# A gated mix of a diagonal state-space layer and a long convolution: taps taken two to a product on half-width tiles, two state tiles placed earlier, C's last tiles loaded ahead of the row loads

## The chip, the cores and the metric

One core of a Trainium2 chip runs the kernel. The metric is the device time of one launch in microseconds; 398.35 us is the median of three runs of the kernel before (398.08 to 398.38). Engines are named as in the profile: PE multiplies matrices (PEld is its weight load), DVE is the vector engine, ACT the scalar engine, POOL the general engine that here mostly issues adding DMAs, SP the engine that issues the plain and the transposing DMAs.

## The reference

The sequence has 2048 steps of 1024 channels. The output is `g * a + (1 - g) * b` with a gate `g` per step. All tensors are bf16 in and out.

```python
x = A_x
g = _sigmoid((x * gate_w).sum(-1, keepdims=True))
# a: diagonal complex state-space layer
for t in range(L):
    h = Lam_bar[None, :] * h + Bu[:, t, :]        # Bu = x @ B_bar^T
y = 2.0 * einsum("blp,dp->bld", hseq, Cmat).real + x * Dskip
# b: k is filtered with 4 taps per channel, multiplied by v, and convolved over the whole length
for t in range(ks):
    k_shift = k_shift + k_pad[:, t:t + S, :] * shift_k[:, ks - 1 - t][None, None, :]
kv = k_shift * v
y = irfft(rfft(kv_pad) * rfft(kf_pad))[:S] + kv * ssm_D
return q * y                                       # q is x
```

The state `h` is complex and has 1024 channels; its recurrence runs over all 2048 steps. `Cmat` is turned first (multiplied by a complex factor per state channel), so that the factor of `B_bar` need not be applied to `Bu`.

## The kernel before

Every instruction goes through a helper (`mm`, `tt`, `ts`, `act`, `move`, `load_t`, `gather`), and `put` fixes the order on each engine to the order in which the program calls them. All rows of the profile therefore have line 94, and they are told apart by tile names. Several sequences are written as generators, and `step` and `run` place their pieces; this is how the order of the work is written by hand.

**The convolution** goes chunk by chunk, 8 chunks of 128 channels (`c` from 0 to 7). For each chunk:

- `load` brings three tiles: `kn` (the long filter, transposed on the way in), `kT` (k transposed: channel on partitions, time along the row, `PAD` zeros in front) and `v`. `kn` and `kT` (and `v` for chunks 0 and 1) share the pool `ld` of three buffers; later `v` tiles hold two chunks each in `xt_pool`. With `held`, ACT first writes one column of the new tile, so that the DMA waits for ACT instead of for every reader of the old tile.
- `taps` computes the 4-tap filter on PE. `dgs` makes four diagonal 128 x 128 matrices, one per tap (channel factors on the diagonal). `tap_sums` takes, for each of 16 blocks of 128 time steps, four products with `kT` (shifted by 0 to 3 steps) as the weights and a diagonal matrix of 128 columns as the moving operand. ACT copies the sums to `ks`.
- `times_v` multiplies by `v` (DVE), mirrors (PE, ACT) and folds the halves (DVE `ev`, and an adding DMA `ks<-lo` from POOL).
- `fold_K`/`mirror_K`, `fwd_K`, `fwd_V` are the forward transforms on PE, copied out by ACT to `Kh` (or the free tiles `BT2`, `BT3`) and `Vh`. `products` multiplies the spectra on DVE, which is most of DVE's work there, about 23 us for a chunk. `inverse` transforms back (`psz`), and SP writes `cv` to a scratch in HBM.

The loop `for c in range(NC - 1)` works on three chunks at once: products of `c`, forward transforms of `n = c + 1`, taps of `nn = c + 2`, and loads of `c + 3`.

**The state layer** has 16 state tiles `(tb, g)`: 4 time blocks `tb` of 512 steps times 4 groups `g` of 256 state channels. `Bu(i)` makes the i-th of them in the sequence `order` from `xT` (x transposed) and `BT` (B transposed), as two halves `j` that I call half tiles; one is some 3.5 us of PE. The first four are `Bu_tile` (products `odd` and `even`, then a small correction with diagonal matrices `lamd`), the others `Bu_plain` (product `both`). Half tiles that do not depend on the convolution fill PE in the loop: 9 of the 32 lie in it, 7 in the last stage (products of chunk 7), and 16 behind it.

**The scans** follow: `scan(tb, g)` on DVE rotates, runs the recurrence, rotates back to `hb`, and adds to `U` what the odd steps lack: four products `q<-hb,lam`, then three sums (`summed`). For the last block's first three scans ACT makes the four products (`Q<-hb,lam`), and the sums are put off until the next scan's recurrence is out (`put_off`). `turn_C` turns a C tile: ACT makes `m`, DVE scales the tile twice and adds `m` (for tiles 4 and 5 an adding DMA adds it). `Cy` and `Cy_group` multiply by C (`psy`, 3.45 us for 128 rows of one group of four); the first four row blocks go row by row (`C0` to `C3`), then by group. The dict `plan` says what PE does behind each scan `j`. `loads(t)` brings a row block's `cv` and x, `scale_b` and `finish` mix it, and SP stores it.

Of the kernel before, what the change touches and what calls it, by code (L numbers as in the profile page):

```python
# [20 lines left out]
def kernel(  # L21
# [153 lines left out]
    def load(which, c, held=False):  # L175
# [7 lines left out]
        elif which == "v":  # L183

            w = 1 if c < 2 else 2
            if w == 1:
                t = ld.tile([128, NT, 1, 128], BF16, name="v", tag="ld")
            else:
                t = xt_pool.tile([128, NT, 2, 128], BF16, name="v2", tag="xT")
            move(t.rearrange("p n k d -> p n (k d)"),  # L190
                 vf.rearrange("(n p) d -> p n d", p=128)[:, :, c * 128:(c + w) * 128])
            for k in range(w):
                lds["v", c + k] = t[:, :, k]
            return
        else:

            t = ld.tile([128, PAD + S], BF16, name="kT", tag="ld")
            put("pool", nc.gpsimd.memset, t[:, 0:PAD], 0.0)
            load_t(t[:, PAD:], kf[:, cc])
        lds[which, c] = t  # L200


    kT0 = ld.tile([128, PAD + S], BF16, name="kT", tag="ld")
    v0 = ld.tile([128, NT, 1, 128], BF16, name="v", tag="ld")
    put("pool", nc.gpsimd.memset, kT0[:, 0:PAD], 0.0)
    for h in range(2):
        hs, ns = slice(h * S // 2, (h + 1) * S // 2), slice(h * NT // 2, (h + 1) * NT // 2)
        load_t(kT0[:, PAD + hs.start:PAD + hs.stop], kf[hs, 0:128])
        move(v0[:, ns, 0], vf.rearrange("(n p) d -> p n d", p=128)[:, ns, 0:128])
    lds["kT", 0], lds["v", 0] = kT0, v0[:, :, 0]  # L210
# [8 lines left out]
    def load_xT(tb, halves=(0, 1), held=False):  # L219
        if 0 in halves:  # L220
            xTs[tb] = (xt_pool if tb in (1, 2) else xt_first).tile([128, ND, TB], BF16, name="xT", tag="xT")
# [61 lines left out]
    gwb = consts.tile([128, ND], BF16, name="gwb")  # L283
    psp = ps2([128, 2, 512], "p")
# [184 lines left out]

    def of_blocks(ks, h):  # L470
# [5 lines left out]
    def taps(c, dg):  # L476
        kT = lds.pop(("kT", c))
# [204 lines left out]
    def lam_diag(g, home, on_act=False):  # L682

        t = lamd[g] = home.tile([128, 2, 3, 128], BF16, name=f"lamd{g}", tag=f"lamd{g % 2}")
# [8 lines left out]
    def Bu(i):  # L693
        tb, g = order[i]
        if i in (10, 11):
# [3 lines left out]
        else:  # L699
# [3 lines left out]
            else:  # L703
                home = uu[0 if i in (0, 1, 13, 14) else 1] if i < 6 or i in (13, 14) else s5p["uu"]
# [10 lines left out]
        return [Bu_tile(tb, g, U, j, (i, j) == (2, 1)) for j in range(2)]  # L715

    def Bu_tile(tb, g, U, j, halved):
# [3 lines left out]
        for a in (1, 0):  # L721
# [5 lines left out]
            if a == 1:  # L727
# [3 lines left out]
                if halved:  # L731
                    yield
# [42 lines left out]
    put_off = []  # L775

    def scan(tb, g, fin):
# [7 lines left out]
        for js in ([slice(0, 1), slice(1, 2)] if last else [slice(0, 2)]):  # L785
# [38 lines left out]
            by_act = tb == NTB - 1 and not last  # L824
            if by_act:
# [175 lines left out]
    old = ahead = none  # L1001
    tiles = (b for i in range(6) for b in Bu(i))

    for c in range(NC - 1):
# [6 lines left out]
        if c == 0:  # L1011
# [22 lines left out]
            load_xT(0)  # L1034
            lam_diag(0, lam_pool, True)
            continue
        if c == 1:
            load("v", 4)
# [11 lines left out]
        if c == 2:  # L1050
            load("v", 6)
        if nn < NC:
            dg = dgs(nn)
        bu = next(tiles) if c == 4 else ahead if c == 6 else none
        step(bu)
        fwd_K(n, (0, 1))
        step(bu)
        fwd_K(n, (2, 3))
        if c == 6:
            load_xT(2, held=True)  # L1060
# [18 lines left out]
        bu = [next(tiles) for _ in range({1: 1, 2: 1, 3: 1, 5: 1, 6: 3}.get(c, 0))] + [none, none]  # L1079
        if c == 5:  # L1080
            bu[1] = ahead = next(tiles)
        step(bu[0])
        fwd_V(n, (0, 1))
        if nn + 1 < NC:
            load("kn", nn + 1, True)
            load("kT", nn + 1)
        if c in (1, 2):
            load_BT(1, c - 1)
        elif c in (3, 4):
            load_xT(1, (c - 3,))  # L1090
        step(bu[0])
        step(bu[1])
        fwd_V(n, (2, 3))
        if bu[1] is not ahead:
# [265 lines left out]
```

## Time and profile before

| | |
|---|---|
| time, median of 3 | 398.35 us |
| the profiled execution: time | 400.61 us |
| the profiled execution: span from first to last instruction | 398.8 us |
| granted PE clock over the span | 0.996 |
| HBM read and written | 12.86 MB and 8.39 MB |

The share of busy time by stage, in us, from the windows of the trace:

| stage (us from the start) | length | PE | DVE | ACT | DMA share |
|---|---|---|---|---|---|
| start, chunk 0 (0 to 45) | 45 | 42.34 | 39.78 | 34.68 | 0.93 |
| loop, c = 1 to 5 begun (45 to 163) | 118 | 115.86 | 116.28 | 97.47 | 0.67 to 0.85 |
| c = 6 (163 to 187) | 24 | 23.17 | 23.90 | 16.00 | 0.69 |
| products of chunk 7 (187 to 224) | 37 | 37.00 | 36.66 | 19.57 | 0.81 |
| first scans (224 to 266) | 42 | 39.92 | 39.95 | 37.08 | 1.11 |
| scans and row blocks (266 to 394) | 128 | 127.77 | 118.86 | 82.64 | 0.75 to 1.01 |

A DMA share near or above 1 means that the 16 DMA engines had work queued throughout. Two engines, PE and DVE, are each busy nearly all of the span, and the rows must be read for which of them is waited for at a given place.

### The profile page before, as it was taken

What the parts mean: (1) busy time and instruction counts of PE and PEld (TensorE: products, weight loads), DVE (VectorE), ACT (ScalarE), POOL (GpSimd) and SP (SyncE); (2) the same over time, 40 slices, a digit from 0 to 9 for tenths busy, and PEclk for the clock granted to TensorE, in tenths of its full rate; (3) what the DMA queues carried; (4) which work ended last, traced back from release to release, by engine and by line L of the source; (5) the groups of instructions that cost most, each with busy time, mean ns of one, the idle gap of its engine ahead of it and who ended that gap; (6) DMA issues with size and microseconds to landing.
All of it is one profiled execution on the core that took longest, in us unless ns stands there. A gap on an engine that the chain in (4) does not pass through costs nothing.

```text
span 398.8 us, 6544 instructions
## 1 busy us (share of the span) xinstructions
PE 386.1 (97%) x2437; PEld 206.0 (52%) x2437; DVE 376.8 (94%) x610; ACT 287.4 (72%) x434; POOL 72.2 (18%) x96
## 2 busy tenths in 40 slices
PE   8999899999999999999999999979999999999995
PEld 5456357474656647566444444424444444444442
DVE  8799999999999999999999899999999999999944
ACT  4797995969878796765429799936978874996201
POOL 3011030200202011020001010503344233433000
PEclk9999999999999999999999999989999999999999
DMA  7969993996929398097994799978999998988402
GB/s 160 159 142 223 205 261 70 231 213 138 210 58 230 56 156 190 28 156 113 209 204 88 180 196 188 195 164 167 199 188 178 253 261 142 218 163 170 121 0 106
DMA packets 129601, 65.72 MB, mean 165 GB/s; under 512 B 106393, under 2 KB 113313, under 8 KB 129570
## 3 DMA queue, kind: packets, MB, share of 16 engines
q1 hardware_dynamic: 117664, 42.22, 48.7%
q0 software_dynamic: 11824, 23.07, 33.8%
q8 instruction: 19, 0.31, 0.3%
q14 instruction: 12, 0.10, 0.1%
q10 hardware_dynamic: 82, 0.02, 0.0%
HBM read 12.86 MB, written 8.39 MB: 53 GB/s over the span
## 4 chain that ended last, share of the span: by engine, by line
PE 68%; DVE 19%; ACT 6%; issue 4%; DMA 2%; POOL 0%; DVEq 0%; ACTq 0%; POOLq 0%
PE psy L94 27%; PE both L94 12%; PE psk L94 7%; PE taps L94 5%; PE psz L94 4%; DVE BT L94 4%; PE psv L94 3%; PE foldk L94 3%; PE even L94 3%; DVE wkh L94 3%; DVE CT L94 2%; ACT Vh L94 2%; PE odd L94 2%; DVE W L94 2%; DMA ks<-lo 2%
## 5 line engine op out<-in xcount | busy, mean ns | idle before, releaser
L94 PEld LDWEIGHTS <-BT 128*128 128x128 bf16 x640 | 62.2, 98 | 47.8
L94 PE MATMUL both<-xT,BT 128*128 128x512 bf16 x384 | 83.7, 379 | 0.0
L94 PE MATMUL psy<-CT,hb 128*128 128x512 bf16 x256 | 59.4, 387 | 2.3 <-DVE CT L94 2.3
L94 PE MATMUL psy<-CT,U 128*128 128x512 bf16 x256 | 57.4, 379 | 0.0
L94 PEld LDWEIGHTS <-hb 128*128 128x128 bf16 x256 | 25.3, 99 | 33.9 <-issue 5.1
L94 POOL DMA_DIRECT2D U<-Q x24 | 23.3, 983 | 100.8 <-ACT Q L94 61.0
L94 ACT ACTIVATE U<-both 128x512 bf16<-128x512 f32 x48 | 26.4, 593 | 20.4 <-PE both L94 20.1
L94 PEld LDWEIGHTS <-U 128*128 128x128 bf16 x256 | 25.1, 98 | 30.2
L94 ACT ACTIVATE Vh<-psv 128x1024 bf16<-128x1024 f32 x32 | 31.0, 1033 | 11.9 <-PE psv L94 11.9
L94 DVE TENSOR_TENSOR_SCAN W<-rv,init,A 128x256 bf16<-128x256 f32 x48 | 32.2, 730 | 0.0
L94 PE MATMUL taps<-dg,kT 128*128 128x128 bf16 x512 | 31.2, 223 | 0.0
L94 POOL DMA_DIRECT2D G<-wkh x8 | 9.7, 1218 | 115.5 <-DVE wkh L94 115.5
L94 PEld LDWEIGHTS <-kT 128*128 128x128 bf16 x512 | 29.8, 100 | 1.0 <-issue 0.2
L94 PEld LDWEIGHTS <-SF 128*128 128x128 bf16 x184 | 18.0, 98 | 20.0 <-issue 1.5
L94 PE MATMUL psk<-eok,SF 128*128 128x512 bf16 (+1 forms) x120 | 28.1, 354 | 0.0
L94 ACT ACTIVATE Q<-U,lam 128x512 bf16<-128x512 bf16 (+1 forms) x48 | 27.7, 606 | 0.0
L94 PE MATMUL psz<-G,CI 128*128 128x512 bf16 x64 | 24.3, 380 | 2.4 <-DVE G L94 1.9
L94 PE MATMUL psz<-G,SI 128*128 128x512 bf16 x64 | 24.3, 379 | 0.0
L94 DVE TENSOR_TENSOR wkh<-BT,Vh 128x3072 bf16<-128x3072 bf16 (+4 forms) x20 | 21.8, 1111 | 0.0
L94 DVE TENSOR_TENSOR wkh<-Kh,Vh 128x3072 bf16<-128x3072 bf16 (+2 forms) x16 | 21.3, 1350 | 0.0
L94 ACT ACTIVATE BT<-psy,gcols 128x1024 bf16<-128x1024 f32 x5 | 5.4, 1109 | 21.8 <-PE psy L94 21.8
L94 ACT ACTIVATE m<-psy,gcols 128x1024 bf16<-128x1024 f32 x8 | 8.9, 1113 | 16.6 <-PE psy L94 16.6
(189 smaller groups left out, 780.7 us busy)
## 6 DMA issues: line engine op xcount, KB each, us to landing
U<-Q POOLq DMA_DIRECT2D x24, 256.0 KB, 5.3
G<-wkh POOLq DMA_DIRECT2D x6, 768.0 KB, 8.1
cv_scr<-cv SPq DMA_DIRECT2D x16, 256.0 KB, 2.6
v<-in_B_v_dram SPq DMA_DIRECT2D x3, 1024.0 KB, 9.6
out_dram<-m SPq DMA_DIRECT2D x8, 256.0 KB, 5.6
BT<-cv_scr SPq DMA_DIRECT2D x7, 256.0 KB
out_dram<-BT SPq DMA_DIRECT2D x7, 256.0 KB, 2.0
ks<-lo POOLq DMA_DIRECT2D x6, 256.0 KB, 7.4
```

The costliest lines, as they stand in the source:

```text
L94: i = f(*a, **kw)
```

## The change

- **Taps two to a product.** For chunks 3 to 7, the channels of a chunk are split in two halves of 64. A tile then holds a half twice: on 64 partitions as it is, on the other 64 delayed by two steps. One product over 128 partitions so takes two taps of 64 channels; two products (shift 0 and 1) make the four taps, and the moving operand has 64 columns instead of 128. The number of products stays 4 for a block of 128 steps, 64 for a chunk.
- **Copies.** The second tile `kB` and the delayed halves come from three copies in SBUF, `spread`, issued by SP behind the chunk's `kT` load: two that read the fresh `kT`, and one that overwrites its upper half when these two are done. `kB` takes the third `ld` buffer.
- **Factors.** `pcol2` and `ident2` hold the factors of two taps over a half, made at the start by eight small products, a copy and a sum; `dgs` makes four matrices of 64 columns.
- **Loads.** `v` is loaded chunk by chunk into one tile `v2` for two chunks (the first of them still whole). `kn` and `v` of the next chunk are issued ahead of the taps, `kT` and the copies right behind them; `BT1` and `xT` 1 move with them, and `xT` 2 to the start of `c = 6`.
- **State tiles.** The pieces of the first four tiles (eight half tiles, three pieces each, 24 steps in all) are spread over `c` = 1 to 6, four or five pieces for each `c` (two in `c = 6`), and three half tiles of the next two lie in `c = 6`. So 11 half tiles are in the loop, 6 in the last stage (with `b10`), and the rest behind it; tile 13 moves from behind `C3` to before `C0`.
- **C.** Tiles 0 and 1 are now added by DMA too. Tiles 6 and 7 are turned inside scan 3, and loaded ahead of the rows. The order of the loads is `CT0`, `BT2`, `BT3`, `CT1`, `CT2`, `CT3`, then `CT4`, `CT5` before the inverse of chunk 7.
- **Scans 4 and 9** have their four products made by ACT, as 12, 13 and 14 had already. The products of scan 13 move behind the four copies of group `G23` on ACT.

```diff
+    def spread(c):
+        a, b = lds["kT", c], lds["kB", c]
+        lo, hi, n = slice(0, 64), slice(64, 128), PAD + S
+        move(b[lo, 8:], a[hi, 8:])
+        move(b[hi, 10:], a[hi, 8:n - 2])
+        yield
+        move(a[hi, 10:], a[lo, 8:n - 2])
...
+        for q in range(4):
+            for t in range(2):
+                mm(psp[t * 64:t * 64 + 64, 1, 64 + q * ND:64 + (q + 1) * ND],
+                   skr[:, q // 2 * 64:q // 2 * 64 + 64, q % 2 + 2 * t], ident[32:32 + ND, 32:32 + ND], True, True)
+        copy(pcol2, psp[:, 1, 64:64 + 4 * ND].rearrange("p (i j) -> p i j", j=ND))
+        tt(ident2, ident[:, 0:64], ident[:, 64:128], ALU.add)
...
+    def packed_sums(halves, dg, h):
+        ps = ps2([128, 8, 128], "taps")
+        for n in range(8):
+            for e, k in enumerate(halves):
+                for m in range(2):
+                    k0 = PAD + (8 * h + n) * 128 - m
+                    mm(ps[:, n, e * 64:e * 64 + 64], k[:, k0:k0 + 128], dg[:, e, m], m == 0, m == 1)
+        return ps
...
-            act(of_blocks(ks, h), by_block(tap_sums(kT, dg, h)), func=ACT.Copy)
+            sums = tap_sums(kT, dg, h) if c < 3 else packed_sums((kT, kB), dg, h)
+            act(of_blocks(ks, h), by_block(sums), func=ACT.Copy)
...
+    scaled_by_act = (4, 9, 12, 13, 14)
...
-            by_act = tb == NTB - 1 and not last
-            if by_act:
+            by_act = tb * NG + g in scaled_by_act
+            if tb * NG + g == 3:
+                run(turning[7])
...
     for c in range(NC - 1):
...
+        if c == 6:
+            load_xT(2)
...
             step(fk)
             if c < 5:
                 step(fk)
+            if nn + 1 < NC:
+                load("kn", nn + 1, True)
+                load("v", nn + 1)
+                if c == 1:
+                    load_BT(1, 0)
+                elif c in (2, 3):
+                    load_xT(1, (3 - c,))
+            step(parts)
             taps(nn, dg)
+            if nn + 1 < NC:
+                load("kT", nn + 1, True)
+                apart = spread(nn + 1)
+                step(apart)
+                if c == 1:
+                    load_BT(1, 1)
+                run(apart)
...
-        by_sum = pi in (4, 5)
+        by_sum = pi in (0, 1, 4, 5)
...
-    load_CT(1)
     load_BT(2, 0)
     load_BT(2, 1)
-    load_CT(2)
     load_BT(3, 0)
     load_BT(3, 1)
+    load_CT(1)
+    load_CT(2)
     load_CT(3)
...
+    CT_pool((6, 7), "ctc")
+    load_CT(6)
     loads(0)
...
-    plan = ["B8", "B9 B10", "B11", "B12 C0", "C1", "C2", "C3 B13", "B14 B15", "G10", "G11", "G12 G13", "G20", "G21",
+    plan = ["B8", "B9 B10", "B11", "B12 B13 C0", "C1", "C2", "C3 B14", "B15", "G10", "G11", "G12 G13", "G20", "G21",
             "G22 G23", "", ""]
...
+        if j == 3:
+            run(turning[6])
+        if j == 0:
+            run(turning[1])
...
-                if tl == 1 and put_off:
-                    put_off[-1][0]()
...
+    run(turning[0])
     step(scans[0])
```

More of the change, by code (lines that the diff above doesn't have):

```diff
@@ L694, in Bu @@
         tb, g = order[i]
+        if i == 13:
+            V_ = s5p["v13"].tile([128, 2, 2, HB], BF16, name="V13")
+            O_ = lam_pool.tile([128, 2, 2, HB + 2], BF16, name="O13", tag="lamd")
+            Us[tb, g] = V_, O_[:, :, :, 2:]
+            turns_U[i] = turn_U(g, V_, O_)
+            return [Bu_plain(tb, g, V_, O_, j) for j in range(2)]
         if i in (10, 11):
@@ L999 @@
     fwd_V(0, (2, 3))
-    old = ahead = none
-    tiles = (b for i in range(6) for b in Bu(i))
+    old = none
+    parts = (None for i in range(4) for b in Bu(i) for _ in b)
+    tiles = (b for i in (4, 5) for b in Bu(i))
     for c in range(NC - 1):
@@ L1049 @@
         run(old)
-        if c == 2:
-            load("v", 6)
         if nn < NC:
             dg = dgs(nn)
-        bu = next(tiles) if c == 4 else ahead if c == 6 else none
-        step(bu)
+        if c % 2 == 0:
+            step(parts)
         fwd_K(n, (0, 1))
-        step(bu)
+        if c % 2 == 0:
+            step(parts)
         fwd_K(n, (2, 3))
         if c == 6:
-            load_xT(2, held=True)
             run(sp)
@@ L1078 @@
             step(tv)
-        bu = [next(tiles) for _ in range({1: 1, 2: 1, 3: 1, 5: 1, 6: 3}.get(c, 0))] + [none, none]
-        if c == 5:
[L1081 to L1094, printed above, removed]
-            step(bu[1])
-        run(bu[2] if c == 6 else none)
-        if c == 2:
+            step(parts)
+        else:
+            run(next(tiles))
+            run(next(tiles))
+        fwd_V(n, (0, 1))
+        if c < 6:
+            step(parts)
+            if c in (1, 3):
+                step(parts)
+        fwd_V(n, (2, 3))
+        if c == 5:
+            step(parts)
+        elif c == 6:
+            run(next(tiles))
+        if c == 1:
             lam_diag(1, lam_pool)
@@ L1152 @@
         steps(prod, 3)
-        b0, b1, b2 = tiles
-        run(b0)
+        run(next(tiles))
         run(back)
         gate(1)
-        run(b1)
+        gate(2)
         run(prod)
@@ L1163 @@
         run(turns_U[6])
-        run(b2)
-        gate(2)
         steps(turning[0], 2)
@@ L1168 @@
         run(b8)
-        back = inverse(c)
-        step(back)
-        run(back)
+        steps(turning[1], 2)
         run(b9)
-        steps(turning[1], 2)
+        b10, b11 = Bu(8)
+        run(b10)
+    CT_pool((4, 5), "ctb")
+    load_CT(4)
+    load_CT(5)
+    back = inverse(c)
+    step(back)
+    run(back)
     h3.close()
```

82 lines of the change are left out of this document (51 added, 31 removed).

## The prediction

> **What bounds the kernel now.** I read the page's busy table first, then the chain of waits over the last third, then the timelines of PE and DVE where the chain names them.
>
> ```profile
> PE 386.1 (97%) x2437; PEld 206.0 (52%) x2437; DVE 376.8 (94%) x610; ACT 287.4 (72%) x434; POOL 72.2 (18%) x96
> ```
>
> Two engines fill the span, so shortening one gains only until the other ends last. The chain from 260 us on (start, length, engine and tile):
>
> ```profile
> 264.93 0.02 issue
> 264.96 1.24 DVE CT L94
> 266.19 0.04 issue
> 266.23 23.42 PE psy L94 x100
> 289.65 20.72 PE both L94 x96
> 310.37 0.78 PE p L94 x32
> 311.15 82.92 PE psy L94 x384
> 394.07 0.02 issue
> ```
>
> DVE's turned C tile releases PE at 266.23, and from there PE runs without a gap to 394.07; 4.73 us of last sums and stores follow. The 96 products `both` are six half tiles, 3.45 us each. How far behind is DVE? Its timeline:
>
> ```profile
> 226.72 0.48 DVE L94 TENSOR_SCALAR CT<-CT,c2r 128x1024 bf16<-128x1024 bf16 x1 [1.50 <-ACT m L94]
> ...
> 235.31 1.14 DVE L94 TENSOR_SCALAR q<-hb,lam 128x512 bf16<-128x512 bf16 x4
> ...
> 379.35 0.49 DVE L94 TENSOR_TENSOR hb<-hb,trn 128x256 bf16<-128x256 bf16 x2
> ```
>
> and PE's:
>
> ```profile
> 82.12 3.75 PE L94 MATMUL taps<-dg,kT 128*128 128x128 bf16 x64
> 85.71 1.91 PE L94 MATMUL odd<-xT,BT 128*128 128x256 bf16 x16
> 87.45 1.91 PE L94 MATMUL even<-xT,BT 128*128 128x256 bf16 x16
> ...
> 174.04 0.94 PE L94 MATMUL p<-gwb,xT 128*128 128x1 bf16 x32
> 174.84 1.91 PE L94 MATMUL odd<-xT,BT 128*128 128x256 bf16 x16
> ...
> 380.07 3.62 PE L94 MATMUL psy<-CT,hb 128*128 128x512 bf16 x16
> 383.53 3.62 PE L94 MATMUL psy<-CT,U 128*128 128x512 bf16 x16
> ```
>
> The last `hb` is done at 379.84, and PE begins the last group, which reads it, at 380.07: DVE is only 0.23 us ahead there. That first row block reads the second half of `hb` from its ninth product on, 8 x 0.216 = 1.73 us later. So PE can come forward by 0.23 + 1.73 = 1.96 us alone; all beyond that needs DVE earlier too. In the loop the two are level as well: inverse transforms start at 46.48, 69.63, 93.21, 117.19, 140.35 and 164.41, about 23.5 us apart, of which PE's own work is 23.15 us.
>
> **The change, part by part, for PE.** Start to start, 64 tap products take 85.71 - 82.12 = 3.59 us, 56.1 ns each; 256 columns take 1.74/16 = 109 ns, 512 columns 3.46/16 = 216 ns. That is 0.416 ns a column, so 64 columns should take 56.1 - 26.6 = 29.4 ns: 1.71 us less for a chunk, 8.5 us for five. No row has 64 columns. The bounds are nothing saved (the weight load, as long as before, sets the pace) and 56.1 - 25.0 = 31.1 ns, 9.95 us in all, from the gate's 32 products with one column and a full weight load (174.04 to 174.84, 25.0 ns each). I take 8.5, as that row puts the weight load below 29.4 ns.
>
> By the Trainium skill, "TensorE: Matmul & The Clock Gate", section "Back-to-back issue gap", a stream of weight load and product pairs sustains some 81 ns for 128 columns, set by both operations. By that the pair would be bound by its load and the change would save nothing; the trace's 56.1 ns and 25.0 ns disagree, and I go by them.
>
> The pieces take the room up. Before, `c` = 1 to 4 held one half tile each (3.5 + 0.44 = 3.94 us). Now `c` = 1 and 3 hold odd, even, correction, odd = 1.75 + 1.75 + 0.44 + 1.75 = 5.69, and `c` = 2 and 4 hold 1.75 + 0.44 + 3.94 = 6.13. With 1.71 off, PE's work there changes by +0.04 and +0.48 us: 1.0 us more over four iterations. At `c` = 5 it falls by 1.8 us and at 6 by 1.2 us. In the last stage six half tiles stand ahead of the inverse of chunk 7, as before; but now `b6` is one half tile earlier and needs `BT2`. DVE frees `BT2` at 190.5 as before, its load now follows `CT0` at once (before at 191.90), and lands some 5.1 us after a 1.9 us issue, the second part near 200. PE asks near 197 and waits 1 to 3 us, which the 1.8 us gained in the loop cover: the inverse ends near 219 (219.57 before). Eleven half tiles follow before `C0`, as before. So `C0` starts near 257 (257.56), two half tiles fewer lie behind it (6.9 us), and PE's two waits for C (1.28 and 1.03 us) go, as tiles 6 and 7 are turned within scan 3. PE could end 0.6 + 6.9 + 2.3 = 9.8 us earlier.
>
> **For DVE.** Scans 4 and 9 lose 1.14 us each (4 `q` products): 2.28. Tiles CT0 and CT1 lose the addition, 1.14 us start to start each: 2.28. The start gains a copy and a sum on the critical start, 0.17 us rows both: +0.35. Work: -4.2 us. The wait of 1.50 us for ACT's `m` of CT1 goes, since it is made before `b9` is copied out; what was late behind it was PE's `both` of 219.73, so it doesn't return elsewhere. The loop costs something back: if DVE waits for every bit that PE is longer, 1.0 us, if none, 0; I take 0.5. Sum: 4.2 + 1.5 - 0.5 = 5.2 us earlier.
>
> **Both together.** The end moves by the smaller of 9.8 and 5.2 + 1.96 = 7.16: 7.1 us. The span becomes 398.8 - 7.1 = 391.7. The profiled execution took 400.61 in all, 2.26 above the median; taking 7.1 from the median gives 391.25, and I say 391.3.
>
> **What is costed at nothing, and its cover.** SP issues 15 copies more, two more `v` loads, POOL four more adding DMAs (0.86 to 0.98 us each), ACT ten more activations in scans and holds. ACT has room (72%). On SP the copies wait for the `kT` load, and the last for the first two; behind them stand both parts of `xT` 0 at `c` = 0, the second part of `BT1` at `c` = 1, and always the two `cv` stores, whose tile is needed again 23 us later. The chain from ACT's hold to the last copy is one issue (1.96), one landing (4.6), two copies in a row (256 KB each; `pbb` 4.6): 15.8 us. Least: 1.24 + 4.1 + 2.0 + 2.0 = 9.3; most, with the folding DMA's 9.3 for a copy: 3.7 + 5.8 + 18.6 = 28.1. The cover is one iteration less taps and copy-out, 23.5 - 1.9 - 1.0 = 20.6. At 15.8 there are 4.8 us to spare, so I take nothing.
>
> The Trainium skill, "DMA: Bandwidth & Descriptors", "Specifications", asks for 512 bytes or more in one descriptor; `v` in single chunks has runs of 256. By it a half load would cost up to what a whole one did. The rows here give 4.1 us for 256 KB in 256-byte runs and 9.6 us for 1 MB in 512-byte runs, nearly in proportion to 2 x 4.1 for half the bytes, so the rule holds partly; a `v` load is needed an iteration later, and its sum stays nothing.
>
> **Rivals.**
> - *PE alone sets the end.* If DVE sheds also its small waits (0.62 us twice for `Vh`, 0.55 in the first scans), it is 7.0 us earlier, 8.9 with the half group, and the end moves 8.9 us: 389.5. For: PE is freer at c = 5 and 6. Against: it isn't at c = 1 to 4.
> - *DVE gains only its work.* If every iteration of the loop costs DVE about 0.6 us more, by pieces on ACT between the copies of `Vh`, or if ACT's products for scan 13, now behind four copies that wait for PE, hold DVE by 2 us: 7.1 - 3 = 4.1, giving 394.3. For: loop and tail have no slack on DVE.
> - *The weight load paces the taps.* Then the loop is 1.75, 2.19, 1.75, 2.19 us longer on PE, 7.9 in all, of which DVE at level pegging pays some 7: 5.2 + 0.5 - 7 + 1.96 = +0.7 gained, 397.7 to 398.3, no change. Against: 25.0 ns at the gate.
> - *The copies come late: slower.* PE stands in order before the taps of chunks 3 to 7, and each us beyond the cover costs a us five times, because DVE waits for `ks`. At 22.6 us for the chain the loss is 10 us against 7.1: 401.3. It decides from 22.0 us on (1.4 x 5 = 7.1). For: the DMA share is 1.0 to 1.3 between 30 and 60 us and 0.96 to 1.12 from 70 to 90. Against: it is 0.72 and 0.00 in the ten us after the taps at 60 to 70, just where the chain would run.
>
> **How the numbers follow.** Forecast 391.3, chance 0.53; PE alone 389.5, 0.10; DVE's work only 394.3, 0.18; no gain, 0.06; late copies, 0.13. Faster by over 0.2% (about 0.8 us, what these measurements can tell) holds in the first three: 0.81; within 0.2%: 0.05; slower: 0.14. The range runs from 388.6 (all 9.8 us) to 396.5 (DVE's work only, and two more us lost in the loop); what is left out is the last two cases.
>
> **What would show it.** Right: tap products at about 29 ns; DVE's last `hb` near 374.6 and PE's last group waiting about 2 us for it; `both` rows behind `C0` 64 instead of 96; no wait for CT around 264. Wrong: PE idle in front of `taps` with the copies of `kB` or `kT` as releaser (late copies); tap products still near 56 ns; DVE waiting for `Vh` over 3 us in the loop; a wait for `BT2` beyond 4 us at `b6`.

## The result, and the profile after

The changed kernel takes 414.25 us (median of 4, 411.55 to 418.05) beside 398.37 us of the kernel before on the same chip: 1.0368 times as long, with an interval of 1.0299 to 1.0437. The prediction was 391.3 us. The profiled execution took 413.06 us, its span is 411.3 us and the granted clock 0.973. Kernels of this study scatter by several per cent where the kernel before stays within about one; a ratio below compares undisturbed executions alone, so that it can stand lower than the medians over all runs do, and it is left out where too few were undisturbed.

The page's busy table of the changed kernel:

```profile
PE 382.3 (93%) x2411; PEld 201.5 (49%) x2445; DVE 372.0 (90%) x602; ACT 291.3 (71%) x444; POOL 76.4 (19%) x100
```

PE has 3.8 us less to do than before (386.1) and DVE 4.8 us less (376.8). DVE's work fell as forecast (4.2). PE's figure is rough, since the table lists 2411 products beside 2445 weight loads; what its taps gained is read from their starts below. The kernel is slower because both engines now stand idle: DVE for 39.3 us of the span, where it was 22.0. Where? The changed kernel's timeline for PE, at the taps of chunk 3 (columns: start, length, engine, operation, tiles, count, and in brackets the idle time ahead and who ended it):

```profile
61.10 0.22 PE L94 MATMUL taps<-dg,kT 128*128 128x64 bf16 x2
...
62.96 1.91 PE L94 MATMUL even<-xT,BT 128*128 128x256 bf16 x16
```

Sixty-four tap products from 61.10 to 62.96: 29.1 ns each. Then the next iteration, in the chain of waits of the changed kernel:

```profile
70.62 4.35 DMA kT<-in_B_k_dram
...
76.20 4.42 SPq L94
...
80.73 12.70 DMA kT<-kT
...
93.47 3.07 PE taps L94 x64
```

and PE's timeline just ahead of those taps:

```profile
91.48 1.89 PE L94 MATMUL odd<-xT,BT 128*128 128x256 bf16 x8 [5.72 <-DMA BT<-in_A_B_im_dram]
```

The load of `kT` 4, SP's issue of `BT1`'s second part and the third copy stand one behind the other, 22.8 us from the issue at 70.62 to the last landing at 93.43. The prediction's chain starts earlier, at ACT's hold of the tile, and from there it is 29.4 us, because SP is busy with the loads ahead. ACT's timeline, then SP's:

```profile
64.08 0.20 ACT L94 ACTIVATE kT<-pih 128x1 bf16<-128x1 f32 x1
```

```profile
60.59 4.54 SPq L94 DMA_TRANSPOSE kn<-in_B_ssm_k_dram  x1
...
65.81 4.65 SPq L94 DMA_TRANSPOSE BT<-in_A_B_re_dram  x1
```

PE waits for two things here, one behind the other. `BT1`, which was issued between the copies, holds it in the middle of sixteen `odd` products that began at 84.71; when they are done, the third copy has just landed. Without the wait for `BT1` PE would have reached the taps near 86.5, and the copy alone would have held it 7.0 us. At the taps of chunk 6 PE waits for the third copy itself:

```profile
143.36 0.22 PE L94 MATMUL taps<-dg,kT 128*128 128x64 bf16 x2 [1.24 <-DMA kT<-kT]
```

The windows of 10 us (PE, PEld, DVE, ACT and POOL busy, then PE clock, DMA share, GB/s), first of the kernel before:

```profile
80.00:90.00 10.00, 10.00 (x111) 7.80 (x109) 9.93 (x11) 6.62 (x9) 0.14 (x2) 1.00 0.97 211
```

then of the changed kernel:

```profile
80.00:90.00 10.00, 5.76 (x33) 2.76 (x30) 9.93 (x11) 4.93 (x7) 0.97 (x2) 0.95 1.45 133
90.00:100.00 10.00, 8.36 (x97) 6.44 (x99) 5.28 (x5) 3.55 (x5) 0.11 (x1) 0.71 1.14 236
```

Look at the last two columns together: the DMA engines are busier than before (1.45 against 0.97) and move fewer bytes (133 against 211 GB/s).

A ruler for the loop is the start of DVE's full-width product of spectra, one an iteration:

| kernel | c=0 | 1 | 2 | 3 | 4 | 5 | 6 |
|---|---|---|---|---|---|---|---|
| before | 47.47 | 71.19 | 95.18 | 118.19 | 141.90 | 165.40 | 190.43 |
| changed | 48.14 | 72.13 | 103.49 | 127.04 | 152.47 | 175.97 | 200.98 |

The shift is 0.67, 0.94, 8.31, 8.85, 10.57, 10.57, 10.55 us: 7.4 us are lost around chunk 4's taps and 1.7 around chunk 6's. Behind the loop it grows again. The timelines of ACT and DVE of the changed kernel follow; in that stretch of the kernel before DVE's longest wait is 1.50 us, and ACT waits for no load:

```profile
250.01 1.15 ACT L94 ACTIVATE pbb<-pbb,omg 128x1024 bf16<-128x1024 bf16 x1 [8.76 <-DMA pbb<-cv_scr]
252.82 1.15 ACT L94 ACTIVATE gd<-rows,gcols 128x1024 bf16<-128x1024 bf16 x1 [1.67 <-DMA rows<-in_A_Dskip_dram]
```

```profile
256.08 0.48 DVE L94 TENSOR_SCALAR CT<-CT,c2r 128x1024 bf16<-128x1024 bf16 x1 [9.59 <-ACT m L94]
```

ACT stands 8.8 us at the first row's `pbb`, with `m` of the next C tile behind it, and DVE waits 9.6 us for that `m`. The end is PE's, as before:

```profile
379.18 3.61 PE L94 MATMUL psy<-CT,hb 128*128 128x512 bf16 x16 [0.74 <-ACT BT L94]
```

### The profile page after: what moved, and what is told of

Same layout as the page of the kernel before. It is cut to its first block, busy times and chain, and to the rows that moved or that the text cites. A ratio compares the mean times of both kernels' runs of the same rounds, so it can differ in the third digit from the quotient of the medians.

```text
span 411.3 us, 6567 instructions
## 1 busy us (share of the span) xinstructions
PE 382.3 (93%) x2411; PEld 201.5 (49%) x2445; DVE 372.0 (90%) x602; ACT 291.3 (71%) x444; POOL 76.4 (19%) x100
## 2 busy tenths in 40 slices
DMA packets 135506, 70.72 MB, mean 172 GB/s; under 512 B 114921, under 2 KB 117745, under 8 KB 135474
## 4 chain that ended last, share of the span: by engine, by line
PE 28%; DMA 25%; DVE 17%; issue 12%; ACT 12%; SPq 3%; POOL 2%; DVEq 0%; POOLq 0%; ACTq 0%
DMA U<-Q 7%; PE psy L94 7%; PE both L94 5%; DMA kT<-kT 5%; DVE BT L94 4%; PE psk L94 3%; SPq L94 3%; ACT Vh L94 3%; PE taps L94 3%; DVE wkh L94 3%; PE psv L94 2%; DMA cv_scr<-cv 2%; DMA xlast<-in_A_x_dram 2%; DMA kT<-in_B_k_dram 2%; DMA xT<-in_A_x_dram 2%
## 5 line engine op out<-in xcount | busy, mean ns | idle before, releaser
L94 PE MATMUL both<-xT,BT 128*128 128x512 bf16 x374 | 87.8, 393 | 10.1 <-ACT U L94 8.3
L94 PE MATMUL psy<-CT,hb 128*128 128x512 bf16 x251 | 57.3, 379 | 1.0 <-ACT BT L94 0.7
L94 PE MATMUL psy<-CT,U 128*128 128x512 bf16 x236 | 53.4, 379 | 0.2
L94 ACT ACTIVATE U<-both 128x512 bf16<-128x512 f32 x44 | 24.3, 594 | 19.8 <-PE both L94 19.6
L94 PEld LDWEIGHTS <-U 128*128 128x128 bf16 x240 | 23.5, 98 | 28.3
L94 PE MATMUL taps<-dg,kT 128*128 128x128 bf16 (+1 forms) x352 | 24.9, 222 | 1.4 <-DMA kT<-kT 1.2
L94 ACT ACTIVATE Q<-U,lam 128x512 bf16<-128x512 bf16 (+1 forms) x44 | 25.5, 609 | 0.0
L94 PEld LDWEIGHTS <-kT 128*128 128x128 bf16 x352 | 23.6, 107 | 3.0 <-issue 1.8
L94 DVE TENSOR_TENSOR U<-U,q 128x512 bf16<-128x512 bf16 (+2 forms) x42 | 19.2, 484 | 3.7 <-ACT q L94 3.2
L94 PE MATMUL odd<-xT,BT 128*128 128x256 bf16 x128 | 16.3, 282 | 5.7 <-DMA BT<-in_A_B_im_dram 5.7
```

The lines of the kernel that those rows point to most:

```text
L94: i = f(*a, **kw)
```

## The experiments

All times below are medians, with the range over all runs in brackets; the kernel before took 398.7 to 399.2 us beside them.

**The two losses taken away one at a time.** Four kernels: `nocopy` leaves out the copies, `rows` puts the order of the C loads back, `nocopy_rows` does both, `fulltaps_rows` has neither copies nor packing.

```diff
# nocopy (the tile kB goes too)
-        move(b[lo, 8:], a[hi, 8:])
-        move(b[hi, 10:], a[hi, 8:n - 2])
         yield
-        move(a[hi, 10:], a[lo, 8:n - 2])
...
-            sums = ... packed_sums((kT, kB), dg, h)
+            sums = ... packed_sums((kT, kT), dg, h)
# rows
-    load_CT(4); load_CT(5)     # ahead of the inverse of chunk 7
-    load_CT(6)
     loads(0)
     move(rows_, ...)
-    load_CT(7)
-    load_xT(3)
+    load_CT(4); load_CT(5)
     loads(1)
+    load_xT(3)
+    load_CT(6); load_CT(7)
     loads(2)
# fulltaps_rows, beside both
-            sums = ... packed_sums((kT, kT), dg, h)
+            sums = tap_sums(kT, dg, h)
```

> Leaves out the fifteen delayed half copies of chunks 3 to 7 (the tile kB is gone, both halves of the product read kT), so the output for those taps is not the reference's; loads, products and everything else stay. Theory (two separate losses on the DMA queues: about 8 us in the loop by late copies, about 8 us in the scans by the C loads in front of pbb, rows and Dskip): the shift against the kernel before at the inverse of chunk 5 falls from +10.5 to under +2 us, the scan loss stays, total 402 to 406. Rival (the loads that now come together and early, with v in 256-byte runs, crowd the queue, and the copies only share the queue): the loop loss stays at 6 us or more, total 410 to 415. Rival (one loss only, the late loop pushes the C loads into the scans' loads): both go, total 391 to 395.

> Only the order of the C loads is put back as in the kernel before: rows and pbb first, then CT4 and CT5, then CT6 and CT7. Theory (two separate losses): the store of cv lands within 4 us again, ACT's wait for pbb of 8.8 us and DVE's wait for m of 9.6 us go, the loop loss of 10.5 us stays: 403 to 407. Rival (the wait in the scans comes from a late loop alone, so the order of loads hardly matters): 411 to 416. Rival (C tiles now come late for the turns and give the gain back): DVE waits for m or CT in scans 3 to 6, 408 to 413.

> Both edits: leaves out the fifteen delayed half copies (output for those taps not the reference's) and puts the order of the C loads back. Theory (both losses are independent and there is no third): 391 to 396, faster than before, as the prediction's sum had it. Rival (a third loss, scans 9 and 4 with ACT's products, or the tiles moved into the loop): 397 to 403.

> No copies, four tap products of 128 columns as in the kernel before for all chunks, order of the C loads put back; the rest of the change stays. Theory: the packing is worth 1.7 us of PE a chunk, of which DVE lets through at most half: 395 to 400, 2 to 7 us over the run without copies that keeps the packed products. Rival (the packing is worth nothing, since DVE sets the end): within 1 us of that run.

`nocopy`: 402.2 (394.25 to 411.1), ratio 0.9934 (0.9886 to 0.9983). Its ruler reads 47.79, 71.77, 95.08, 118.33, 142.31, 165.80, 190.81: the loop loses 0.4 us in place of 10.5, as my theory had it. The same loop without copies loses 1.3 us in `nocopy_ct6` and 2.6 in `nocopy_rows`, so the copies cost some 8 to 10 us of the 10.5. In all `nocopy` is 12 us under the changed kernel by the medians and 17 by the ratios, more than the loop alone; where the rest comes from was not taken apart. Of the loss in the scans ACT's wait is left (the trace does not name its releaser; the load of `pbb` was issued at 231.78):

```profile
236.15 1.15 ACT L94 ACTIVATE pbb<-pbb,omg 128x1024 bf16<-128x1024 bf16 x1 [6.47 <-issue]
```

`rows`: 420.93 (401.61 to 423.61), above all three forecasts, and `nocopy_rows`: 404.57 (398.74 to 413.21), ratio 1.0086 (1.0046 to 1.0126), another miss. What the third forecast for `rows` named is in its trace: ACT waits 9.10 us for a C tile, and DVE 7.80 for ACT. But its loop also loses 16.4 us, more than the changed kernel's 10.5, so its time does not tell what the order of the loads costs. ACT's timeline of `nocopy_rows`, profiled in its longest run (413.21):

```profile
262.38 2.19 ACT L94 ACTIVATE m<-CT,mc2i 128x1024 bf16<-128x1024 bf16 x2 [12.18 <-DMA CT<-in_A_C_im_dram]
```

`fulltaps_rows`, profiled at 408.1, shows the same waits for C tiles with 4.42 and 3.30 us; ACT of the kernel before has none. So my theory of the second loss was too simple: the old order of loads feeds the rows and starves tiles 6 and 7, which the change turns earlier. `fulltaps_rows`: 410.36 (406.33 to 413.92), ratio 1.018 (1.0134 to 1.0227), above its 395 to 400, but 5.8 us over `nocopy_rows` by the medians and 3.7 by the ratios: the packing is worth something when it is free.

**Other orders of the loads.** `bt_last` moves the second part of `BT1` behind the third copy; `nocopy_ct6` leaves out the copies and puts only CT6 behind the first row's loads, CT4 and CT5 staying early; `bt_ct6` makes both moves and keeps the copies.

```diff
# bt_last
                 step(apart)
-                if c == 1:
-                    load_BT(1, 1)
                 run(apart)
+                if c == 1:
+                    load_BT(1, 1)
# nocopy_ct6
-    load_CT(6)
     loads(0)
     move(rows_, ...)
+    load_CT(6)
     load_CT(7)
```

> One load is moved: the second part of BT 1 follows the third copy of chunk 4 on SP instead of standing between the second and the third. Theory (the copies are late because other transfers stand between and beside them in SP's queue, most of all this one, after whose 4.4 us issue the third copy took 12.7 us): chunk 4's copies are in place some 8 us earlier, the 7.4 us lost at chunk 4's taps fall to under 2, those of chunk 6 (1.7 us) stay; time 404 to 409. Rival (the third copy is slow by itself, as it moves within one tile): it takes over 8 us again and the loss stays, 410 to 416.

> Without the fifteen half copies (output for those taps not the reference's) and with the loads of cv, x and rows for the first row ahead of CT6; CT4, CT5 stay early. Theory (in the scans there is one demand too many on SP's queue: with CT6 first, pbb is late by 6.5 us, with all C tiles behind, CT6 is late by 12 us; this middle order feeds both in time): ACT's wait for pbb under 2.5 us, DVE's wait for m under 2 us, time 391 to 397, against 402.2 without this edit. Rival (the queue is full whatever the order, something else is then late by as much): 400 to 405.

> The changed kernel with both moves of loads, nothing left out. Theory: both losses go but for chunk 6's, 394 to 401, about as the kernel before. Rival (the copies themselves crowd the queue in every chunk): 403 to 410.

`nocopy_ct6` came as forecast in some of its runs, 398.7 (395.62 to 407.89), ratio 0.9969 (0.9930 to 1.0009), span of the profiled execution 394.8: ACT's wait for `pbb` is 1.83 us and DVE's for `m` 1.91. By the ratios it can't be told from `nocopy` (0.9934), so that shorter waits made the kernel faster is not shown. Its order of loads is that of most runs below. The two with copies missed: `bt_last` 415.24 (403.71 to 426.39), `bt_ct6` 414.27 (407.13 to 416.87), ratio 1.0269 (1.0155 to 1.0384). In `bt_last`, profiled in its shortest run, the third copy is issued at 78.60, 2.1 us earlier, but then `BT1` takes 8.14 us to issue and PE waits for it, not for a copy. SP's timeline of `bt_last`:

```profile
78.60 0.46 SPq L94 DMA_DIRECT2D kT<-kT  x1
79.11 8.14 SPq L94 DMA_TRANSPOSE BT<-in_A_B_im_dram  x1
```

In `nocopy` the same issue took 1.99 us. Who is late changes with the order; that something is late does not.

**Is it the wait for the copies, or their traffic?** `unread_ct6` issues every copy and lets nothing read it; `noshift_ct6` does the same with copies that stay in their half of the partitions; `no_third_ct6` leaves out the third copy of each chunk; `poolq_ct6` issues them on POOL's queue; `poolcopy_ct6` lets GpSimd copy, without any transfer. All have CT6 behind the first row's loads.

```diff
# unread_ct6
-        move(a[hi, 10:], a[lo, 8:n - 2])
+        move(b[hi, 10:], a[lo, 8:n - 2])
...
-            sums = ... packed_sums((kT, kB), dg, h)
+            sums = ... packed_sums((kT, kT), dg, h)
# noshift_ct6, beside that
+        move(b[lo, 8:], a[lo, 8:])
+        move(b[hi, 10:], a[hi, 8:n - 2])      # twice, for the second and the third
# poolq_ct6 (poolcopy_ct6: nc.gpsimd.tensor_copy), all three copies
-        move(b[lo, 8:], a[hi, 8:])
+        put("pool", nc.gpsimd.dma_start, out=b[lo, 8:], in_=a[hi, 8:])
```

> All fifteen copies are issued and move their bytes, but the taps read kT alone and no instruction waits for a copy (the third writes kB in place of kT); the output for the delayed taps is not the reference's. The first row's loads stand ahead of CT6, as in the run without copies that took 398.7 us. Theory A (the copies' traffic slows the transposed loads of kn, BT and xT that share SP's queue, and PE waits for those as well): the loop still loses 5 us or more, with PE waiting for BT or xT; 404 to 412. Theory B (the taps' own wait for the chain of load and copies is what costs): the loop loses under 2 us, 396 to 401.

> As unread_ct6 (nothing waits for a copy but the next user of its tile, the output for the delayed taps is not the reference's), but each copy stays in its own half of the partitions. Theory (bytes and descriptors cost, not the crossing): 405 to 425 as unread_ct6's 418. Rival (crossing halves is what slows the transfers): loop loss under 2 us, 397 to 402.

> The third copy of each chunk is left out (the output for two delayed taps of half the channels is not the reference's); the first two stay and the taps wait for them; first row's loads ahead of CT6. Theory (the third copy is the one that meets the transposed loads of the next chunk, as kn and BT took 8 to 12 us to issue right behind it): loop loss under 2 us, 397 to 402. Rival (every copy beside a transposed load costs): loop loss 4 us or more, 403 to 412.

> Nothing left out: the copies are issued on POOL's DMA queue in place of SP's. Theory A, if it is the one ring that the transposed loads share with the copies: BT's second part takes some 2 us to issue again in place of 4 to 9, loop loss under 3 us, 396 to 402. If it is the 16 engines behind both rings: the loss stays, 405 to 415. Theory B (chain of waits): the chain is as long, so the loss stays, 405 to 415; POOL's other transfers may come later too.

> Nothing left out: GpSimd itself copies the half tiles (fifteen copies of 64 x 2056 elements) and no transfer is added. Theory A: transposed loads as fast as without copies, and if a POOL copy takes under 4 us the taps wait for nothing: 394 to 401. It fails if the copies are slow (over 5 us each, 15 us a chunk) or slow DVE down, with which POOL shares its access to the memory as far as any run here may show: 402 to 420.

`unread_ct6`: 418.3 (407.49 to 426.59); even its shortest run lies 8.8 us above the median of `nocopy_ct6`. Nothing computes with the copies, and in the profiled run (415.11) the loop loses 18.6 us by its end, more than the changed kernel's 10.5. PE's timeline and the windows of this run:

```profile
101.15 1.89 PE L94 MATMUL odd<-xT,BT 128*128 128x256 bf16 x8 [11.45 <-DMA BT<-in_A_B_im_dram]
```

```profile
90.00:100.00 10.00, 0.00 (x0) 0.00 (x0) 7.48 (x8) 0.00 (x0) 0.00 (x0) 0.71 1.22 81
```

`BT1`'s second part was issued at 80.86 and PE gets it at 101.15. From 90 to 100 us PE does nothing, the DMA engines are full (1.22) and move 81 GB/s. The expectation was wrong in one thing: a copy is still waited for, by the tile that takes over the buffer of `kB`, the next `kn`. ACT's timeline:

```profile
102.53 0.20 ACT L94 ACTIVATE kn<-pih 128x1 bf16<-128x1 f32 x1 [12.75 <-DMA kB<-kT]
```

That wait ends 1.4 us behind PE's, while PE is at its eight `odd` products (101.15 to 103.04) and ACT has nothing of them to copy out yet, so it's the load of `BT1` that holds the loop here. That is theory A: the traffic does this harm without the taps' own wait. `noshift_ct6`, 413.08 (403.98 to 414.54), shows the same in the profiled run (414.54) with PE waiting 12.23 us for `xT` at 74.97, so the crossing of halves is not needed for it. `no_third_ct6`, 413.78 (411.16 to 416.24), ratio 1.0354 (1.0273 to 1.0436), misses my forecast: ten copies do as much harm as fifteen. SP's timeline and PE's in that run:

```profile
85.77 15.35 SPq L94 DMA_TRANSPOSE kn<-in_B_ssm_k_dram  x1
```

```profile
96.45 1.89 PE L94 MATMUL odd<-xT,BT 128*128 128x256 bf16 x8 [10.88 <-DMA BT<-in_A_B_im_dram]
```

`poolq_ct6`: 415.75 (411.81 to 417.14), ratio 1.0405 (1.0337 to 1.0473). SP's timeline:

```profile
73.95 2.03 SPq L94 DMA_TRANSPOSE BT<-in_A_B_im_dram  x1
...
114.08 15.46 SPq L94 DMA_TRANSPOSE xT<-in_A_x_dram  x1
```

`BT1` is issued in 2.03 us (it stands ahead of the first copy there), and at `c` = 2 the ruler stands 2.1 us behind the kernel before in place of 8.3. An iteration later `xT` takes 15.46 us to issue, DVE waits 12.04 us for POOL's `G<-wkh`, and POOL's `ks<-lo`, issued at 110.16, lands after 16.49 us, where the median before was 7.4. So SP's own queue is not what is full: the loss moves, but it stays without any copy in that queue. The Trainium skill, "DMA: Bandwidth & Descriptors", section "Issuing engines are not separate DMA queues", says that transfers run on the same 16 engines whoever issues them, and that a second issuer saves only issue time; this run agrees.

`poolcopy_ct6`: 431.39 (428.91 to 440.05), ratio 1.0792 (1.0733 to 1.0851), slower than all of these. Its POOL timeline, then SP's:

```profile
76.93 3.92 POOL L94 COPY kB<-kT 64x2056 bf16<-64x2056 bf16 x2 [9.87 <-DMA kT<-in_B_k_dram]
80.91 17.57 POOL L94 COPY kT<-kT 64x2054 bf16<-64x2054 bf16 x1
```

```profile
74.53 2.05 SPq L94 DMA_TRANSPOSE BT<-in_A_B_im_dram  x1
```

The first two copies take 1.96 us each, the third 17.57, and POOL's adding transfer, for which DVE waits 8.22 us, stands behind them. Why the third was so slow was not tried. The run settles another question. It keeps the third tile, `kB`, in the three buffers of `ld`, as the runs with copies do, but adds no transfer, and `BT1`'s second part is issued in 2.05 us: the fuller buffers alone do not stretch an issue.

**The same bytes without a chain.** `four_ct6` loads each half twice from HBM, transposed, 64 columns at a time, so that no copy is needed (for `c` from 3 on).

```diff
-            load_t(t[:, PAD:], kf[:, cc])
...
+                for e, u in enumerate((t, b)):
+                    src = kf[:, c * 128 + e * 64:c * 128 + e * 64 + 64]
+                    load_t(u[0:64, PAD - 2:PAD - 2 + S], src)
+                    load_t(u[64:128, PAD:], src)
```

> Nothing left out: the half tiles of chunks 3 to 7 come by four transposed loads of 64 columns from DRAM each, in place of one transposed load of 128 and three copies that wait for it and for one another, and the first row's loads stand ahead of CT6. Theory (what costs is the chain of waits on SP, load then copies): no chain is left, so the taps wait for nothing, 391 to 398. Rival (what costs is the bytes and descriptors of the extra transfers beside the loads): transposed loads take longer than copies, kn and v come late, 405 to 420.

It took 3662.38 us (3643.93 to 3671.58). The instructions on `kT` and the DMA view of this run:

```profile
L94 SPq DMA_DIRECT2D kT<-in_B_k_dram x10: 657/84160/172531, 40.4 to 2763.3; - x10
```

```profile
DMA packets 2745666, 69.40 MB, mean 19 GB/s; under 512 B 2726041, under 2 KB 2728865, under 8 KB 2745634
```

The loads are no transposes any more: they stand as plain transfers, with 2.75 million packets in place of 135,506, and SP issues one for up to 172.5 us. The Trainium skill, the same page, section "Constraints" under "DMA Transpose (X-bar)", says that inputs with fewer than 128 in the free dimension can fall back to a rearranged access; with 64 columns that is what the trace shows. The question of the chain was not answered by it.

**Where the copies do harm.** `packed57_ct6` packs chunks 5 to 7 alone; `fulltaps_ct6` packs none.

```diff
# packed57_ct6
-            if c >= 3:
+            if c >= 5:
                 lds["kB", c] = ...
...
-            sums = tap_sums(kT, dg, h) if c < 3 else packed_sums((kT, kB), dg, h)
+            sums = tap_sums(kT, dg, h) if c < 5 else packed_sums((kT, kB), dg, h)
```

> Nothing left out: chunks 3 and 4 use four products of 128 columns, only chunks 5 to 7 are packed with copies; first row's loads ahead of CT6. Theory (the copies do harm where BT 1 and xT 1 are loaded beside them, chunks 4 and 5 above all): chunk 4's stall goes, chunk 5's and 6's stay at 1 to 3 us, PE's longer taps cost some 3 us: 402 to 408. Rival (nine copies cost three fifths of fifteen): 407 to 412.

> Nothing left out: no packing, no copies, first row's loads ahead of CT6. Against the run without copies that keeps the packed products (398.7): 3 to 8 us slower, 402 to 407, if PE's 8.5 us count in the loop, where the moved pieces already stand; within 1 us of it if DVE sets the pace there.

`packed57_ct6`: 403.75 (400.22 to 414.65), ratio 1.0106 (1.0066 to 1.0145); its ruler from `c` = 2 on reads 98.77, 122.02, 146.00, 169.50, 194.53, that is 3.3 us behind `nocopy_ct6` (95.51, 118.76, 142.74, 166.23) all along and 2.8 at the end (191.75). Two chunks that are not packed cost PE 3.5 us (3.59 us for 64 tap products of 128 columns, 1.86 for 64 of 64 columns), so in this execution, the shortest of the ten, the nine copies of chunks 5 to 7 cost the loop nothing. `BT1` is in by then, and one half of `xT` 1; that this is the reason is argued, not shown. By the ratios the kernel is 5.5 us over `nocopy_ct6`, so that in other runs some 2 us may be the copies'. `fulltaps_ct6`: 405.52 (404.40 to 406.80), ratio 1.0139 (1.0075 to 1.0204): 6.8 us more than `nocopy_ct6`, which is what the packed products save when no copy is paid for.

**DVE's relief.** `nocopy_ct6_s49` gives the products of scans 4 and 9 back to DVE. `before_sum` is the kernel before with only the additions of CT0 and CT1 given to adding transfers, `before_sum49` the same with scans 4 and 9 on ACT as well.

```diff
# nocopy_ct6_s49
-    scaled_by_act = (4, 9, 12, 13, 14)
+    scaled_by_act = (12, 13, 14)
# before_sum, on the kernel before
-        by_sum = pi in (4, 5)
-        if by_sum:
+        by_sum = pi in (0, 1, 4, 5)
+        if pi in (4, 5):
# before_sum49, beside it
-            by_act = tb == NTB - 1 and not last
-            if by_act:
+            by_act = tb * NG + g in (4, 9, 12, 13, 14)
+            if by_act and tb == NTB - 1:
```

> Without the copies (output for those taps not the reference's), first row's loads ahead of CT6, and the q products of scans 4 and 9 on DVE again. Theory (ACT's eight products more stand ahead of its scaling of the rows, whose sums DVE then waits for at scans 6 and 11, 3.0 and 2.0 us, so the 2.3 us saved come back): those waits fall under 1 us and the time is within 1 us of 398.7. Rival (DVE's saving is real and the waits come from late loads): the waits stay and it is 2 to 3 us slower, 400 to 402.

> The kernel before with one part of the change: the additions of the first two turned C tiles are made by adding transfers, nothing else is moved. By the prediction's step (DVE sheds 2.28 us in front of the scans, and PE's two waits for C tiles of 1.28 and 1.03 us lie behind it): 396.0 to 397.5, against 398.7 for the kernel before. Rival (the transfers, at 5 to 10 us each, crowd POOL's queue, or what stands behind C's wait on ACT comes as late as before): 398.3 to 400.

> As before_sum, and the q products of scans 4 and 9 go to ACT as in the change. By the prediction's step (another 2.28 us of DVE, with DVE 0.23 us ahead of PE at the end): 1.5 to 2.3 us under before_sum. By what the run with these products back on DVE showed (ACT scales the rows later, DVE waits for their gathers): within 0.8 us of before_sum, or slower.

`nocopy_ct6_s49`: 399.36 (395.42 to 405.56), ratio 0.9981 (0.9939 to 1.0024), within 0.7 us of 398.7: eight products fewer on DVE are worth nothing that these runs can tell. DVE's wait at scan 6 in `nocopy_ct6`

```profile
288.00 0.69 DVE L94 TENSOR_TENSOR BT<-BT 128x1024 bf16<-128x1024 bf16 x1 [3.04 <-issue]
331.02 0.69 DVE L94 TENSOR_TENSOR U<-U,q 128x1024 bf16<-128x1024 bf16 x1 [2.04 <-ACT q L94]
```

falls to 1.66 us, and that at scan 11 goes. Together that is 3.4 us, more than the 2.28 us saved, so the saving came back as these two waits.

`before_sum`: 407.94 (405.21 to 410.39), ratio 1.0227 (1.0179 to 1.0275). One part of the change that was priced as a gain of 2.28 us costs some 9 us by itself. SP's timeline, first of the kernel before, then of `before_sum`, at tiles 4 and 5:

```profile
225.81 2.22 SPq L94 DMA_TRANSPOSE CT<-in_A_C_im_dram  x1
...
229.42 1.88 SPq L94 DMA_TRANSPOSE CT<-in_A_C_im_dram  x1
```

```profile
225.33 5.10 SPq L94 DMA_TRANSPOSE CT<-in_A_C_im_dram  x1
...
232.54 6.71 SPq L94 DMA_TRANSPOSE CT<-in_A_C_im_dram  x1
```

Four adding transfers of 256 KB are issued by POOL from 223.81 on. The two `im` loads beside them take 5.10 and 6.71 us to issue, the next C tiles come late (ACT waits 7.10 us for one until 268.94), and the windows from 230 to 240 us move 152 GB/s at a share of 1.25, where the kernel before moved 201 at 1.23. It looks like the loop's loss again, with other transfers, but here a wait is mixed in: ACT waits 1.58 us, until 238.53, for an adding transfer itself, which holds `m` until it has landed. The packed runs without copies have these adding transfers too, in another order of the C loads, and stay within 1% of the kernel before; what the transfers cost there was not taken apart. `before_sum49`: 410.49 (400.85 to 416.42), ratio 1.0116 (1.0060 to 1.0172), by its ratio less slow than `before_sum`, by its median more; whether the products on ACT help there can't be told from these runs.

By the ratios only `nocopy` is faster than the kernel before beyond its interval, and it is not the whole computation.

## Why the prediction was wrong

The step that failed is "What is costed at nothing, and its cover". It put the chain from ACT's hold to the last copy at 15.8 us, against a cover of 20.6, and took nothing for the copies, though its own upper bound of 28.1 lay beyond the cover. In the changed kernel the chain took 29.4 us at chunk 4 and 23.8 at chunk 6 (hold at 119.47, landing at 143.22), where PE was ready for the taps 22.4 and 22.7 us behind the hold. So the cover was about right and the chain too short. At chunk 4 it left out 6.3 us in which SP issues the loads ahead and the 4.42 us of `BT1`'s issue between the copies, and the third copy took 12.70 us where the sum had 4.6, from `pbb`. Nor did the step ask what fifteen copies and four more adding transfers do to the transposed loads beside them: where no tap waits for a copy, those loads come late instead. The runs put some 8 to 10 us of the loop on the copies, and some 9 us on the adding transfers when they are added to the kernel before by themselves. Of these it counted POOL's 0.86 to 0.98 us each; in the changed kernel they land after 10.3 us in the median.

- *Tap products* were right: 29.1 ns where 29.4 was forecast, from rows of 128, 256 and 512 columns, with a row of one column as the bound. The rival in which the weight load paces them falls. What the 8.5 us of PE are worth without copies is 6.8 us (`fulltaps_ct6` to `nocopy_ct6`).
- *The state tiles in the loop* were about right: 0.5 us was taken for the loop, and the runs without copies show 0.4 to 2.6.
- *The wait of 1 to 3 us for `BT2` at `b6`* didn't come: between a wait of 1.29 us for `xT` at 186.84 and one of 8.33 us for ACT's `U` at 257.32, PE's timeline shows none.
- *PE behind `C0`* was right in size: in `nocopy_ct6` 130.5 us lie from `C0` (264.28) to the end of the span, before 141.2 (257.56 to 398.8), 10.7 us less where 6.9 and 2.3 were forecast. But `C0` starts 7 us later than the 257 of the sum: the inverse ends at 222.61 instead of 219, and then come waits of 0.64, 1.66 and 0.90 us. So the profiled `nocopy_ct6` spans 394.8 and not 391.7. In the changed kernel 130.5 us lie behind `C0` as well; it starts at 280.85, 23.9 us later than the sum had it. The inverse ends 12.6 us later than forecast, at 231.56, and PE's wait of 8.33 us for ACT's `U` follows.
- *DVE's work* fell by 4.8 us (4.2 forecast), but no run shows any of it at the end. The terms of 2.28 us each were work, and were priced as path. With scans 4 and 9, ACT scales the rows later and DVE waits for them; with CT0 and CT1, the transfers delay the next C tiles. The rival "DVE gains only its work" named ACT as the risk, at scan 13, and still forecast a gain of 4.1 us.
- *The order of the C loads* was not priced at all. CT6 in front of the first row cost ACT 6.5 to 8.8 us at `pbb`; the old order costs it 4.4 to 12.2 us at CT6, since tiles 6 and 7 are turned earlier. These are waits; what they cost in time was not told apart.
- *The rival "copies come late: slower", 401.3*, had the direction and the sign to look for, the third copy as releaser of the taps, and a chain beyond the 22.0 us from which it decides. It had the mechanism half. The loss comes at two chunks and not five times over, and where no tap reads the copies (`unread_ct6`) it stays. Its "against", a DMA share of 0.72 and 0.00 behind the taps, was read from the kernel before, where nothing had yet been moved into that gap; from 60 to 70 us the changed kernel has 1.12.

Why the DMA engines move fewer bytes in such stretches stays open. Such stretches come without the crossing of halves, without the third copy and with either issuing queue; each slow stretch that I read has transposed loads together with added transfers. Where the loss falls also differs: beside chunk 4's copies in the changed kernel, chunk 3's in `noshift_ct6`, chunk 5's in `poolq_ct6`.

## What to carry to other kernels

In this kernel a transfer added where transposed loads are in flight was not priced by its own landing time: what counted as well was how late the loads beside it came, and a landing taken from another stretch of the old profile says nothing about that. Start the chain where the wait starts, count what the issuing queue still has to do ahead of it, and treat an upper bound beyond the cover as a cost. Read the DMA share and the GB/s together, window by window, and leave the new transfers out in a run (or issue them and read nothing) before arguing about who waits for whom. Work taken off an engine is a gain only if what replaces it, here transfers and another engine's queue, is as early as the work was.

## What the hardware showed unexpectedly

- Full DMA engines can move little: 1.45 at 133 GB/s in the changed kernel, 1.22 at 81 in `unread_ct6`, where 0.97 carried 211 GB/s before. SP's issue of one transposed load then stretches from some 2 us to as much as 15.46.
- A transposed load of 64 columns ran in about one packet per element: the twenty loads hold 2.62 million elements, and the run has 2.61 million packets more than the changed kernel. The ten into `kT`, of 256 KB each, landed after 258.0 us in the median, where the kernel before has 4.6 for 128 columns.
- One GpSimd copy of 64 x 2054 elements took 17.57 us, its two predecessors of nearly the same size 1.96 us each.
- The granted clock is slow to come back: in the changed kernel the 64 tap products behind PE's idle stretch of 5.72 us take from 93.47 on 3.07 us by the chain, where those of chunk 3 took 1.87, and the window from 90 to 100 us has a clock of 0.71.
